# An attention and MLP kernel: the first batch opens with two query tiles of 128, its later queries load behind the values, and ties in the instruction order are broken by a hash

## The chip, the cores and the metric

The kernel runs on one core of one Trainium2 chip. The metric is device time in microseconds of one execution, 278.24 us before the change (median of 3 runs, 277.3 to 278.42). The core has TensorE (matrix products, PE in the profile), VectorE (DVE), ScalarE (ACT), GpSimd (POOL) and the queue engine SyncE (SP); loads can be issued from SP, ACT and POOL.

## The reference, cut to what matters

Four batches of eight heads, 768 tokens, head size 64. Attention under a block mask, then an MLP with a squared relu over all 3072 tokens.

```python
scores = scale * np.matmul(q, k.transpose(0, 1, 3, 2))          # q, k, v: (4, 8, 768, 64) f32
mask = np.abs(blk_i - blk_j) <= window                          # blocks of 32, window 1
mask = mask | (blk_i == 0) | (blk_j == 0) | (blk_i == n_blocks - 1) | (blk_j == n_blocks - 1)
... # and 3 sampled key blocks for each query block
scores = np.where(mask, scores, -1000000000.0)
attn = softmax(scores)                                          # written out in the reference
x = (attn @ v).transpose(0, 2, 1, 3).reshape(3072, 512)
h = x @ w_in                                                    # (512, 2048)
r = np.maximum(h, 0.0)
g = r * r
return (g @ w_out).astype(np.float32)                           # (2048, 512)
```

## The kernel before

Heads are taken in pairs; a pair of a batch is a unit `u` (16 units, 4 of each batch). A unit's keys lie on the partitions, 128 at a time, so scores come out as keys x queries, go through the exponential on ScalarE and are the stationary operand of the product with the values; a column of ones in the values gives the row sums. Queries are taken 256 at a time:

```python
QW = 256
def scores(slots, add, e):                    # one slot: unit u, query tile qi, key chunks 2*cp and 2*cp+1
    for a in slots:
        u, qi, cp = a
        ps = ps_s.tile([P, 2, 2, QW], F32, name="ps", tag="ps")          # two of these in all
        for c in range(2):
            for h in range(2):
                nc.tensor.matmul(ps[:, h, c, :], QK[i][hs, 1, ksl], QK[i][hs, 0, qsl], ...)   # L359
            for h in range(2) if add else ():
                nc.tensor.matmul(ps[:, h, c, :], oh[hs, ksl], R2[hs, qsl], ...)   # L363: adds the mask
def exps(a, e):
    A.activation(out=pT, in_=stile.pop(a), func=AF.Exp, scale=scale)     # L369
def masks(a, e):
    V.tensor_tensor(out=pT, in0=pT, in1=m[...], op=AOP.mult)             # L376: where no mask was added
def values(a, e):
    nc.tensor.matmul(po[:, qc, h, :], pT[:, h, c, ...], VT[i][:, h, n, 0:VW], ...)   # L392
def normalize(u, qi, e): ...                  # L399 and L401, VectorE
```

In batch 0 the first query tile has its mask added in the scores by TensorE; for the others a mask of zeros and ones is multiplied in by VectorE. The attention result is transposed (by TensorE in batch 0, by DMA later) into `xT`, and the MLP takes it tile by tile: 256 tokens in batch 0, 384 later.

```python
TILES = [(0, qi * QW, QW) for qi in range(NQ)]
TILES += [(b, c0, S // 2) for b in range(1, B) for c0 in (0, S // 2)]
def hidden(T, f, half, e):                    # ph, L437: 4 matmuls for one f of 16
    nc.tensor.matmul(ph, w_in_sb[:, kc, f * P:(f + 1) * P], xT[b][:, kc, c0:c0 + w], ...)
def relu(T, f, e): ...                        # r, VectorE (L446) or ScalarE (L444)
def square(T, f, e): ...                      # g, GpSimd (L455) or ScalarE (L453)
def output(T, i, ts, cs, part, e):            # py, L477: 2 of 16 f in each part
    nc.tensor.matmul(ytile[T, i], gtile[T, f][:, ts * P:(ts + 1) * P], w_out_sb[:, f, cs[0]:cs[1]], ...)
```

Loads of batch 0 are issued at the start from SP and ACT, whole tensors of 384 KB. The weights come in 8 chunks, 4 of w_in and 4 of w_out, issued by GpSimd; a copy on GpSimd in front of them holds them back until the keys of unit 2 have landed. Three tiny stores on SP ("gates") wait each for a weight chunk and so hold back the loads of the next batch that stand behind them.

```python
load(0, (sy, sc_, sy))                        # queries, keys, values: from SP, ACT, SP
load(1, (sc_, sy, sc_))
load(2, (sy, sc_, sy))
load(3, (sc_, sy, sy))
def w_load(i, e):
    if i == 0:
        G.tensor_copy(out=held, in_=raw[2][1][0:1, 0, 0, 0:2])           # keys of unit 2
    G.dma_start(out=w_in_sb[:, :, fs], in_=wiv[:, :, fs])                # or a chunk of w_out
def loads_gate(i, e):                         # i = 2 (w_in), 5 and 7 (w_out)
    sy.dma_start(out=scratch[0:1, i % 4:i % 4 + 1], in_=src)             # src lies in weight chunk i
```

The order of the instructions on each engine is made ahead, when the kernel is built: every piece of work is a task with durations, dependencies, buffers and a key; of those that could start earliest the one with the smallest key is taken. Twelve matmuls on a constant (`junk`, L223) run at the start. Identity, one-hot rows `oh` and the mask rows `bm` are made on GpSimd and VectorE.

Of the kernel before, what the change touches and what calls it, by code (L numbers as in the profile page):

```python
# [19 lines left out]
P = 128  # L20
# [5 lines left out]
def kernel(  # L26
# [31 lines left out]
    N_WARM = 12  # L58
# [16 lines left out]

    tasks = []
# [3 lines left out]
    AHEAD = {"PE": 0, "DVE": 0, "ACT": 0.2, "POOL": 0.0, "SP": 0.0}  # L80
    LEAD = 14
    PACE0, PACE, SINGLE, MASK_AT = 44, 1.313, 1, 12.0

    class Buf:
        def __init__(self, pool):
            self.pool, self.holds, self.free = pool, 0, 0.0

    class Task:
        def __init__(self, engs, key, fn, deps=(), get=(), put=(), after=0.0, mode=None, dma=0.0, late=None, bias={}, port=False):
            self.engs = engs if isinstance(engs, dict) else dict([engs])  # L90
            self.key, self.fn = key, fn
            self.deps, self.get, self.put = list(deps), list(get), list(put)
            self.after, self.mode, self.dma, self.late, self.bias = after, mode, dma, late, bias
            self.port = port
            self.end = self.eng = None
            self.order = len(tasks)
            for b in self.put:
                b.holds += 1
            tasks.append(self)
# [99 lines left out]

    sy, sc_ = nc.sync, nc.scalar  # L200
    sb_i = consts.tile([nb, n_rand * 2], I32, name="sb_i")
    sy.dma_start(out=sb_i, in_=sampled_blocks.bitcast(I32))
    load(0, (sy, sc_, sy))
    load(1, (sc_, sy, sc_))
    load(2, (sy, sc_, sy))
    load(3, (sc_, sy, sy))
# [7 lines left out]
    warm = consts.tile([P, 512], BF, name="warm")  # L214
# [7 lines left out]
    for _ in range(N_WARM):  # L222
        nc.tensor.matmul(junk, warm[:, 0:P], warm, start=True, stop=True)  # L223
# [7 lines left out]
    G.iota(row, pattern=[[0, 1]], base=0, channel_multiplier=1, **small)  # L231
    o3 = oh.rearrange("a (n p) -> a n p", p=P)
# [4 lines left out]
    identb = consts.tile([P, P], BF, name="identb")  # L237
    make_identity(nc, identb)
# [19 lines left out]
    A.copy(out=oh[D:P, :], in_=oh[0:D, :])  # L258
# [13 lines left out]
    def mask_rows(e):  # L272
        mtile["R"] = ps_s.tile([P, 1024], F32, name="pb", tag="ps")
        for c0 in (0, 512):
            w = min(512, S - c0)
            nc.tensor.matmul(mtile["R"][:, c0:c0 + w], bm, oh[0:nb, c0:c0 + w], start=True, stop=True)

    def mask_rows_evac(c0, c1, e):
        copy(e, R2[:, c0:c1], mtile["R"][:, c0:c1])
# [15 lines left out]
    mtile, cast, ttile = {}, {}, {}  # L295

# [31 lines left out]
    def w_load(i, e):  # L328
        if i == 0:
            G.tensor_copy(out=held, in_=raw[2][1][0:1, 0, 0, 0:2])  # L330
# [18 lines left out]
    def scores(slots, add, e):  # L349
        for a in slots:  # L350
            u, qi, cp = a
            i = u % NPB
            ps = ps_s.tile([P, 2, 2, QW], F32, name="ps", tag="ps")
            qsl = slice(qi * QW, (qi + 1) * QW)
            for c in range(2):
                ksl = slice((cp * 2 + c) * P, (cp * 2 + c + 1) * P)
                for h in range(2):
                    hs = slice(h * D, (h + 1) * D)
                    nc.tensor.matmul(ps[:, h, c, :], QK[i][hs, 1, ksl], QK[i][hs, 0, qsl],  # L359
                                     start=c == 0, stop=not add, skip_group_check=True)  # L360
                for h in range(2) if add else ():
                    hs = slice(h * D, (h + 1) * D)
                    nc.tensor.matmul(ps[:, h, c, :], oh[hs, ksl], R2[hs, qsl],  # L363
# [3 lines left out]
    def exps(a, e):  # L367
        pT = work.tile([P, 2, 2, QW], BF, name="pT", tag="pT", bufs=PT_BUFS)
        A.activation(out=pT, in_=stile.pop(a), func=AF.Exp, scale=scale)  # L369
        ptile[a] = pT  # L370

    def masks(a, e):
        u, qi, cp = a
        pT = ptile[a]
        m = MK[:, cp * 2:cp * 2 + 2, qi * QW:(qi + 1) * QW]
        V.tensor_tensor(out=pT, in0=pT, in1=m[:, None].broadcast_to([P, 2, 2, QW]), op=AOP.mult)  # L376

    def outs_of(t):
        return t[:, 0:4 * VW].rearrange("p (c h d) -> p c h d", h=2, d=VW)

    def values(a, e):
        u, qi, cp = a
        i = u % NPB
        pT = ptile.pop(a)
        if cp == 0:
            otile[u, qi] = ps_o.tile([P, 512], F32, name="po", tag="po")
        po = outs_of(otile[u, qi])
        for c in range(2):
            n = cp * 2 + c
            for qc in range(2):  # L390
                for h in range(2):
                    nc.tensor.matmul(po[:, qc, h, :], pT[:, h, c, qc * P:(qc + 1) * P], VT[i][:, h, n, 0:VW],  # L392
# [3 lines left out]
    def normalize(u, qi, e):  # L396
        po = outs_of(otile[u, qi])
        rs = work.tile([P, 2, 2, 1], F32, name="rs", tag="rs")
        V.reciprocal(out=rs, in_=po[:, :, :, D:VW])  # L399
        xq = work.tile([P, 2, 2, D], BF, name="xq", tag="xq", bufs=XQ_BUFS)  # L400
        V.tensor_tensor(out=xq, in0=po[:, :, :, 0:D], in1=rs.broadcast_to([P, 2, 2, D]), op=AOP.mult)  # L401
        xtile[u, qi] = xq

    def x_transp(u, qi, e):
        xq = xtile.pop((u, qi))
        pt = otile[u, qi][:, 384:512].bitcast(BF)
        for qc in range(2):
            nc.tensor.transpose(pt[:, qc * P:(qc + 1) * P], xq[:, qc].rearrange("p h d -> p (h d)"), identb)  # L408

    def x_evac(u, qi, e):  # L410
# [3 lines left out]
        copy(e, xT[b][:, a, qi * QW:(qi + 1) * QW], otile.pop((u, qi))[:, 384:512].bitcast(BF))  # L414

    def x_transp_dma(u, qi, e):
        b, a = divmod(u, HP)
        if b not in xT:
            xT[b] = work.tile([P, HP, S], BF, name="xT", tag="xT", bufs=XT_BUFS)
        sy.dma_start(out=xT[b][:, a, qi * QW:(qi + 1) * QW].rearrange("r (c p) -> r c p", p=P),  # L420
                     in_=xtile.pop((u, qi)).rearrange("p c h d -> p (c h d)"), transpose=True)
        otile.pop((u, qi))
# [4 lines left out]
    TILES = [(0, qi * QW, QW) for qi in range(NQ)]  # L427
    TILES += [(b, c0, S // 2) for b in range(1, B) for c0 in (0, S // 2)]
    NY = 8

    def hidden(T, f, half, e):
        b, c0, w = T
        if half == 0:
            htile[T, f] = ps_h.tile([P, TWM], F32, name="ph", tag="h")[:, 0:w]
        ph = htile[T, f]
        for kc in range(half * KM // 2, (half + 1) * KM // 2):
            nc.tensor.matmul(ph, w_in_sb[:, kc, f * P:(f + 1) * P], xT[b][:, kc, c0:c0 + w],  # L437
                             start=(kc == 0), stop=(kc == KM - 1))

    def relu(T, f, e):  # L440
        r = work.tile([P, TWM], F32, name="r", tag="r", bufs=R_BUFS)[:, 0:T[2]]
# [7 lines left out]
    def square(T, f, e):  # L449
        g = work.tile([P, TWM], BF, name="g", tag="g", bufs=G_BUFS)[:, 0:T[2]]  # L450
# [5 lines left out]
        gtile[T, f] = g  # L456
# [33 lines left out]
    def T_(engs, key, f, *args, **kw):  # L490
        return Task(engs, key, (lambda e: f(*args, e)), **kw)

    arrive = [(6.2, 6.2, 8.4), (8.4, 10.5, 10.5), (12.5, 12.5, 13.6), (13.6, 15.2, 16.3)]

    order = [(a, qi, cp) for qi in range(NQ) for a in range(HP) for cp in range(CP)]
    order += [(b * HP + a, qi, cp) for b in range(1, B) for qs in ((0, 1), (2,)) for a in range(HP) for qi in qs
              for cp in range(CP)]
    first = {}
    for s, (u, qi, cp) in enumerate(order):
        first.setdefault(u, s)  # L500
    ev, cv, tr, sc_of, va_of, mu, mk, wl, gate, xb = {}, {}, {}, {}, {}, {}, {}, {}, {}, {}

    def prepare(u):
# [5 lines left out]
        if u >= HP:  # L509
# [4 lines left out]
            for w in (1, 0):  # L514
                qc = Buf("qc")
                c = T_({"DVE": 0.55, "POOL": 1.2}, 101, cast_qk, u, w, slice(0, NCH), bias={"POOL": 0.5}, get=[qc], port=True,
                       after=PACE0 + PACE * (s0 - HP * NQ * CP) - LEAD, **at)
                tr[u].append(c)
                ev[u][w, 0] = ev[u][w, 2] = T_(("SP", 1.0), s0 - 10, transp_dma, u, w, deps=[c] + old_s, put=[qc], dma=1.2)
        else:  # L520
            at = dict(after=arrive[u][2])
            for ns in (slice(0, 2), slice(2, NCH)) if u == 0 else (slice(0, NCH),):
                n = ns.stop - ns.start
                for w in (0, 1):
                    qc, hb = Buf("qc"), Buf("h")
                    opts = {"ACT": 0.23 + 0.1 * n} if u == 0 and w else {"DVE": 0.07 + 0.08 * n}
                    if u:
                        opts["POOL"] = 1.2
                    c = T_(opts, s0 - 6 + ns.start, cast_qk, u, w, ns, after=arrive[u][w], get=[qc], port=True)
                    tr[u].append(c)  # L530
                    t = T_(("PE", 0.06 * n), s0 - 5 + ns.start, transp, u, w, ns, deps=[c], get=[hb], put=[qc], mode=128)
                    opts = {"DVE": 0.14 + 0.07 * n}
                    if u == 0:
                        opts["ACT"] = 0.23 + 0.1 * n
                    x = T_(opts, s0 - 4 + ns.start, evac, u, w, ns, deps=[t], put=[hb])
                    for j in range(ns.start, ns.stop, 2):
                        ev[u][w, j] = x
            for w in (0, 1):
                ev[u].setdefault((w, 2), ev[u][w, 0])
        cv[u] = [T_({"POOL": 0.83, "DVE": 0.55}, s0 - 2 if u < HP else 101, cast_v, u, bias={"DVE": 0.6},  # L540
                    deps=at.get("deps", []) + old_v, after=at.get("after", 0.0), port=True)]
        if u == HP - 1:
            for i in range(2 * NWP):
                wl[i] = T_(("POOL", 0.85), -50 + i, w_load, i, after=12.6, late=2.2, dma=2.65)
# [3 lines left out]
    def attend(group, add):  # L548
        s = min(order.index(a) for a in group)
        bufs = {a: Buf("ps") for a in group}  # L550
        sc = T_(("PE", (0.44 if add else 0.22) * len(group)), s, scores, group, add,
                deps=[ev[u][w, 2 if n else 0] for u, qi, cp in group for w, n in ((0, qi), (1, cp))]
                + (mr[:1 + (group[0][1] > 0)] if add else []) + sc_all[-1:], get=[bufs[a] for a in group], mode=64,
                after=PACE0 + PACE * (s - HP * NQ * CP) if s >= HP * NQ * CP else 0.0)
        sc_all.append(sc)
        for a in group:
            u, qi, cp = a
            sc_of[u].append(sc)
            s = order.index(a)
            pt = Buf("pT")  # L560
# [132 lines left out]
```

The softmax here doesn't subtract the row's maximum and nothing guards it: scores larger than these inputs give would overflow.

## Time and profile before

| | |
|---|---|
| time, median of 3 runs | 278.24 us |
| span of the profiled execution | 275.2 us |
| TensorE busy | 263.5 us, 96% |
| ScalarE busy | 212.0 us, 77% |
| VectorE busy | 198.0 us, 72% |
| GpSimd busy | 77.3 us, 28% |
| HBM read, written | 27.26 MB, 6.29 MB |

How to read it: the row of busy shares is over the whole span, and the stages differ. The view of busy time by stretches has one line for each stretch, with the busy time of PE, PEld (weight loads), DVE, ACT and POOL in this order, the number of instructions in brackets, then the granted clock of TensorE, the mean share of the 16 DMA engines and GB/s. A line of the timeline of an engine has start, length, engine, line of the kernel, operation, output and input, shapes, and the number of instructions merged; in brackets what the engine was idle for before it and what ended that. SPq and POOL lines with DMA_DIRECT2D are issues of a transfer, not the transfer.

### The profile page before, as it was taken

How to read it: one execution, taken by the hardware profiler on the slowest of the kernel's cores; microseconds unless marked ns; L12 is line 12 of the kernel's file. 1: busy time of each engine (PE TensorE's matmuls, PEld its weight loads, DVE VectorE, ACT ScalarE, POOL GpSimd, SP SyncE). 2: the span in 40 equal slices, each digit the busy share in tenths (PEclk: the TensorE clock that was granted, in tenths of full speed). 3: DMA queues.
4: the chain of work that ended last, by engine and by line, in shares of the span. 5: the costliest groups of instructions: out<-in, count | busy, mean ns of one | idle time of the engine just before them, and what ended most of it. 6: DMA issues, size and time to landing. Idle time of an engine off the chain costs nothing.

```text
span 275.2 us, 7001 instructions
## 1 busy us (share of the span) xinstructions
PE 263.5 (96%) x2812; PEld 156.7 (57%) x2850; DVE 198.0 (72%) x392; ACT 212.0 (77%) x315; POOL 77.3 (28%) x105
## 2 busy tenths in 40 slices
PE   7897999899999999999999999999999999999994
PEld 2565756567666655655555555555555655555543
DVE  6794799989989778898987768876876745444400
ACT  4688999899899799997898988889989743444311
POOL 4660655625441224453232420111110100010010
PEclk9999999999999999999999999999999999999999
DMA  7999997999979969413512611111022011111122
GB/s 251 376 233 206 267 278 252 262 280 285 318 104 255 206 174 247 154 57 69 117 48 48 137 21 50 57 21 49 12 60 58 12 48 39 40 38 38 40 76 76
DMA packets 50522, 36.89 MB, mean 134 GB/s; under 512 B 30906, under 2 KB 47546, under 8 KB 50490
## 3 DMA queue, kind: packets, MB, share of 16 engines
q1 hardware_dynamic: 44906, 30.29, 41.3%
q0 software_dynamic: 4224, 4.19, 9.2%
q10 hardware_dynamic: 1360, 1.97, 2.1%
q8 instruction: 22, 0.36, 0.5%
q14 instruction: 10, 0.08, 0.1%
HBM read 27.26 MB, written 6.29 MB: 122 GB/s over the span
## 4 chain that ended last, share of the span: by engine, by line
PE 87%; DVE 4%; ACT 3%; DMA 2%; issue 2%; POOL 1%; POOLq 0%; ACTq 0%
PE ph L437 28%; PE py L477 28%; PE po L392 14%; PE ps L359 12%; DMA vs<-in_v_dram 2%; ACT pT L369 2%; PE junk L223 2%; DVE pT L376 1%; PE pt L311 1%; DVE r L446 1%; POOL g L455 1%; DVE QK L182 1%; PE po L408 1%; PE ps L363 0%; ACT MK L291 0%
## 5 line engine op out<-in xcount | busy, mean ns | idle before, releaser
L369 ACT ACTIVATE pT<-ps 128x1024 bf16<-128x1024 f32 x144 | 139.2, 1022 | 9.0 <-PE ps L359 5.6
L437 PE MATMUL ph<-xT,w_in_sb 128*128 128x384 bf16 (+1 forms) x576 | 107.0, 308 | 0.2
L376 DVE TENSOR_TENSOR pT<-pT,MK 128x1024 bf16<-128x1024 bf16 x132 | 98.8, 769 | 10.5 <-ACT pT L369 10.3
L477 PE MATMUL py<-w_out_sb,g 128*128 128x512 bf16 (+1 forms) x362 | 96.2, 369 | 2.5 <-POOL g L455 0.9
L455 POOL TENSOR_TENSOR g<-r 128x256 bf16<-128x256 f32 (+1 forms) x59 | 50.0, 853 | 164.5 <-DVE r L446 134.6
L437 PEld LDWEIGHTS <-w_in_sb 128*128 128x128 bf16 x576 | 51.9, 97 | 33.0 <-issue 1.3
L446 DVE TENSOR_SCALAR r<-ph 128x384 f32<-128x384 f32 (+1 forms) x96 | 49.6, 519 | 28.5 <-PE ph L437 27.2
L453 ACT ACTIVATE g<-r 128x384 bf16<-128x384 f32 (+1 forms) x85 | 42.3, 501 | 29.2 <-DVE r L446 28.5
L392 PEld LDWEIGHTS <-pT 128*128 128x128 bf16 x1152 | 44.4, 98 | 22.4 <-issue 7.7
L392 PE MATMUL po<-VT,pT 128*128 128x65 bf16 x1152 | 53.9, 194 | 1.5 <-DVE xT L182 0.7
L477 PEld LDWEIGHTS <-g 128*128 128x128 bf16 x400 | 36.3, 97 | 24.7 <-POOL g L455 1.2
L359 PE MATMUL ps<-QK 64*128 64x256 bf16 x576 | 46.6, 272 | 0.1
L359 PEld LDWEIGHTS <-QK 64*128 64x128 bf16 x576 | 22.8, 94 | 24.1 <-issue 20.7
L444 ACT ACTIVATE r<-ph 128x384 f32<-128x384 f32 (+1 forms) x48 | 21.0, 445 | 5.3 <-PE ph L437 4.7
L401 DVE TENSOR_TENSOR xq<-po,rs 128x256 bf16<-128x256 f32 x48 | 20.4, 424 | 1.7
L399 DVE RECIPROCAL rs<-po 128x4 f32<-128x4 f32 x48 | 8.6, 180 | 17.9 <-PE po L392 17.6
L180 ACT COPY ys<-py 128x512 f32<-128x512 f32 (+1 forms) x21 | 11.9, 565 | 11.7 <-PE py L477 11.7
L182 POOL CAST VT<-vs 128x768 bf16<-128x768 f32 x15 | 13.5, 902 | 17.9 <-PE po L392 12.1
L182 DVE CAST qc<-ks 128x768 bf16<-128x768 f32 x14 | 9.5, 682 | 0.0
L182 DVE CAST qc<-qs 128x768 bf16<-128x768 f32 (+2 forms) x13 | 8.6, 666 | 0.8 <-DMA qs<-in_q_dram 0.8
L363 PE MATMUL ps<-R,oh 64*128 64x256 bf16 x48 | 5.9, 269 | 0.0
L223 PE MATMUL junk<-warm 128*128 128x512 bf16 x12 | 4.2, 528 | 1.5 <-DVE warm L215 1.5
(52 smaller groups left out, 61.3 us busy)
## 6 DMA issues: line engine op xcount, KB each, us to landing
out_dram<-ys SPq DMA_DIRECT2D x23, 256.0 KB, 2.2
vs<-in_v_dram SPq DMA_DIRECT2D x15, 384.0 KB, 6.4
qs<-in_q_dram SPq DMA_DIRECT2D x14, 384.0 KB, 4.5
ks<-in_k_dram SPq DMA_DIRECT2D x14, 384.0 KB, 6.4
w_in_sb<-in_moe_w_in_dram POOLq DMA_DIRECT2D x4, 512.0 KB, 10.1
w_out_sb<-in_moe_w_out_dram POOLq DMA_DIRECT2D x4, 512.0 KB, 20.7
ks<-in_k_dram ACTq DMA_DIRECT2D x2, 384.0 KB, 6.0
qs<-in_q_dram ACTq DMA_DIRECT2D x2, 384.0 KB, 5.0
```

The costliest lines, as they stand in the source:

```text
L182: (V if e == "DVE" else G).tensor_copy(out=out, in_=in_)
L359: nc.tensor.matmul(ps[:, h, c, :], QK[i][hs, 1, ksl], QK[i][hs, 0, qsl], start=c == 0, stop=not add, skip_group_check=True)
L369: A.activation(out=pT, in_=stile.pop(a), func=AF.Exp, scale=scale)
L376: V.tensor_tensor(out=pT, in0=pT, in1=m[:, None].broadcast_to([P, 2, 2, QW]), op=AOP.mult)
L392: nc.tensor.matmul(po[:, qc, h, :], pT[:, h, c, qc * P:(qc + 1) * P], VT[i][:, h, n, 0:VW], start=(n == 0 and qc == 0 and h == 0), stop=n ...
L401: V.tensor_tensor(out=xq, in0=po[:, :, :, 0:D], in1=rs.broadcast_to([P, 2, 2, D]), op=AOP.mult)
L437: nc.tensor.matmul(ph, w_in_sb[:, kc, f * P:(f + 1) * P], xT[b][:, kc, c0:c0 + w], start=(kc == 0), stop=(kc == KM - 1))
L444: A.activation(out=r, in_=src, func=AF.Relu)
L446: V.tensor_scalar(out=r, in0=src, scalar1=0.0, scalar2=None, op0=AOP.max)
L453: A.activation(out=g, in_=r, func=AF.Square)
L455: (G if e == "POOL" else V).tensor_mul(out=g, in0=r, in1=r)
L477: nc.tensor.matmul(ytile[T, i], gtile[T, f][:, ts * P:(ts + 1) * P], w_out_sb[:, f, cs[0]:cs[1]], start=(f == 0), stop=(f == NF - 1))
```

## The change

In batch 0 the first 256 queries become two tiles of 128, each slot with three key chunks instead of two (128 x 768 exponentials instead of 128 x 1024), so that the first MLP tile has its input after half as many queries. Both tiles have the mask added by TensorE, as the 256-query tile had before. For a 128-query tile the hidden layer takes two f at once, so that relu and square keep their 256 columns. Loads of batch 0 are cut: of the queries only the first 256 come early, the rest stands behind the last values, and the weights are held back by the values of unit 2 instead of its keys. Keys of unit 0 come in two parts. Identity is made before the one-hot rows; 24 more matmuls on the constant are put where TensorE is expected to wait; constants of the task order change, and every key gets an offset from a hash of the task's number.

```diff
-    N_WARM = 12
+    N_WARM, N_IDLE = 15, 24
+    QT0, ADDED, ALONE = [(0, 128), (128, 128), (256, 256), (512, 256)], (0, 128), (0, 128)
-    PACE0, PACE, SINGLE, MASK_AT = 44, 1.313, 1, 12.0
+    PACE0, PACE, SINGLE, MASK_AT = 35.961, 1.493, 1, 17.0
+    TIES = 515867, 2.374, 2.488
+            self.key += TIES[1 if key < 300 else 2] * tie(self.order)
...
-    load(0, (sy, sc_, sy))
-    load(1, (sc_, sy, sc_))
-    load(2, (sy, sc_, sy))
-    load(3, (sc_, sy, sy))
+    for eng, u, w, ns in ((sc_, 0, 1, KEYS[0]), (sy, 0, 0, QRS[0]), (sc_, 1, 1, ALL), (sy, 0, 1, KEYS[1]),
+                          (sc_, 1, 0, QRS[0]), (sy, 0, 2, ALL), (sc_, 1, 2, ALL), (sy, 2, 1, ALL),
+                          (sy, 2, 0, QRS[0]), (sy, 3, 1, ALL), (sy, 3, 0, QRS[0]), (sy, 2, 2, ALL), (sy, 3, 2, ALL),
+                          (sy, 0, 0, QRS[1]), (sy, 1, 0, QRS[1]), (sy, 2, 0, QRS[1]), (sy, 3, 0, QRS[1])):
+        load_part(eng, u, w, ns)          # w: 0 queries, 1 keys, 2 values
...
-    warm = consts.tile([P, 512], BF, name="warm")
+    warm = consts.tile([P, 256], BF, name="warm")
...                                       # identity moved ahead of the two selects on oh
-    A.copy(out=oh[D:P, :], in_=oh[0:D, :])
+    V.tensor_copy(out=oh[D:P, :], in_=oh[0:D, :])
...
+    idle = ps_y.tile([P, 512], F32, name="idle", tag="y")
+    def keep_warm(e):
+        nc.tensor.matmul(idle[:, 0:256], warm[:, 0:P], warm, start=True, stop=True)
...
-            G.tensor_copy(out=held, in_=raw[2][1][0:1, 0, 0, 0:2])
+            G.tensor_copy(out=held, in_=raw[2][2][0:1, 0, 0, 0:2])
...                                       # scores, exps, masks, values, normalize: by start and width
-    TILES = [(0, qi * QW, QW) for qi in range(NQ)]
+    TILES = [(0, c0, w) for c0, w in QT[0]]
+    def per_unit(T):
+        return 2 if T[2] == P else 1
...                                       # hidden, relu, square take per_unit(T) values of f at once
+    KEYS_OF = {P: [tuple(range(CP)), tuple(range(CP, NCH))], QW: [(2 * c, 2 * c + 1) for c in range(CP)]}
```

## The prediction

> **What bounds the kernel now.** I read the busy shares first, then the busy time by stretches, then the chain that ended last, and last the order of work on each engine in the first 60 us, where the change lies.
>
> ```profile
> PE 263.5 (96%) x2812; PEld 156.7 (57%) x2850; DVE 198.0 (72%) x392; ACT 212.0 (77%) x315; POOL 77.3 (28%) x105
> ```
> ```profile
> 20.00:25.00 5.00, 4.44 (x83) 3.00 (x80) 1.62 (x5) 4.48 (x6) 0.00 (x0) 1.00 1.24 207
> ...
> 50.00:60.00 10.00, 9.09 (x121) 6.17 (x122) 8.56 (x19) 9.18 (x15) 5.86 (x7) 1.00 1.21 238
> ...
> 100.00:150.00 50.00, 49.52 (x570) 28.48 (x577) 43.31 (x79) 45.00 (x65) 19.13 (x21) 1.00 0.45 109
> 150.00:200.00 50.00, 49.58 (x558) 28.17 (x564) 37.59 (x73) 44.41 (x62) 7.98 (x10) 1.00 0.22 53
> ```
>
> From 60 us on TensorE is busy over 98% of every stretch: only less TensorE work can shorten that part. To see what is lost earlier I priced all TensorE work at its steady pace, from the chain: hidden matmuls 8 in 0.87 us (256 wide) and 4 in 0.65 (384), output 8 in 1.73 (512), values 16 in 0.59, scores 8 in 0.54; transposes 0.06 each. With the counts of the program: hidden 83.3, output 82.9, values 42.6, scores with added masks 42.1, transposes and mask tiles 6.4, together 257.4 us. I then laid that running sum beside the start times of the weight loads (2850 of 2851 are recorded). Time minus work done, "lost" below, is 5.7 us at the first useful matmul, 7.1 at 7.8 us, 8.9 at 20, 11.1 at 28, 11.4 at 37, 12.6 at 43, 14.0 at 52, and still 14.0 at 271.3 us, the last matmul. So **after 52 us nothing is lost**; span = 257.4 + 14.0 + 3.9 for the last store. All the change can win is part of the 14.0.
>
> The loss has three parts. Until 8 us the data and the masks aren't there. From 8 to 28 us scores wait for ScalarE's exponentials and there is no hidden work to fill in:
>
> ```profile
> 8.77 2.88 ACT L369 ACTIVATE pT<-ps 128x1024 bf16<-128x1024 f32 x3 [1.65 <-PE ps L363]
> ...
> 18.41 5.61 ACT L369 ACTIVATE pT<-ps 128x1024 bf16<-128x1024 f32 x6 [1.30 <-PE ps L363]
> ```
> ```profile
> 27.64 1.71 PE L437 MATMUL ph<-xT,w_in_sb 128*128 128x256 bf16 x12
> ```
>
> The hidden layer starts at 27.64 us, when four head pairs times three exponentials are through. From 35 to 50 us VectorE and ScalarE are both over 90% busy in every 5 us, and from 37 to 52 us 2.6 us more go. Beside all this runs the DMA, saturated to 41 us:
>
> ```profile
> 11.07 0.17 POOL L330 COPY held<-ks 1x2 f32<-1x2 f32 x1 [0.92 <-DMA ks<-in_k_dram]
> 11.20 3.36 POOL L333 DMA_DIRECT2D w_in_sb<-in_moe_w_in_dram  x4
> 14.54 2.98 POOL L336 DMA_DIRECT2D w_out_sb<-in_moe_w_out_dram  x4
> ```
> ```profile
> 23.88 0.25 SPq L343 DMA_DIRECT2D scratch<-w_in_sb  x1
> ...
> 34.69 0.24 SPq L343 DMA_DIRECT2D scratch<-w_out_sb  x1
> ...
> 41.39 0.24 SPq L343 DMA_DIRECT2D scratch<-w_out_sb  x1
> ```
>
> These small stores are gates: each goes out the moment a weight chunk has landed. So w_in chunk 2 is there at 23.9 us, w_out chunk 1 at 34.7, w_out chunk 3 at 41.4. The packet records give all eight: 18.5, 21.0, 23.6, 26.3 (w_in), 29.6, 34.4, 37.6, 41.1 (w_out). Chunks alone take 2.55 us; w_out 1 took 4.7 because batch 1's first loads, let go by the gate at 23.9, ran beside it.
>
> [...] Here chunk w_in 2's last packet ended at 22.6 and its semaphore came at 23.6, so 1.0. [...] The trace has 216 at 512 (8 in 1.73 us). [...]
>
> **The change part by part.**
> (1) *TensorE work.* Hidden for the two 128-query tiles: 128 matmuls at 0.06 [...] = 7.7 for 64 x 0.109 = 7.0: +0.7. Scores and added masks: 192 of 128 columns, two side by side, at 0.03 (half of 0.055, the pace of a 256-wide one with masks) = 5.8 for 96 x 0.0675 = 6.5: -0.7. Sum 0. The 24 idle matmuls (0.108 each, 2.6 us) stand where the order expects TensorE to wait.
> (2) *Opening.* First keys 196 KB and queries 131 KB instead of 393 KB each; identity built before the selects; no table load behind a fifth load on ScalarE's queue. First scores near 6.2 us instead of 8.12, loss there 5.8 instead of 7.3: -1.5.
> (3) *Exponentials.* 128x512 took 0.60 us and 128x1024 took 1.02, so 128x768 takes 0.81, in a row 0.73 against 0.935. The first hidden matmul stands behind about 14 of them: 14 x 0.73 = 10.2, copies and masks on ScalarE 1.2, waits for keys of pairs 1 to 3 about 2, from 6.9 us: 20.3, plus 0.7 to the matmul: 21.0 us. Work ahead of it is 13.0 us, so the loss is 8.0 there, against 11.1 before. Up to here **3.1 us are won**.
> (4) *Weights.* Here I expect most of it to be given back. The weights are now held by the values of pair 2. Bytes ahead of those and with them: 4.72 MB of loads less 0.39 and 1.05 = 3.28 MB, at the 0.35 MB/us of the loads before (4.72 MB from 1.9 to 15.4 us): 11.3, landed 11.7, then their cast on GpSimd 0.9: first weight issue about 12.7 instead of 11.2. Before, chunk 0 shared 0.8 us with the last value load; now it doesn't. Net **1.1 us later** for every chunk: 19.6, 22.1, 24.7, 27.3, 30.7, 35.5, 38.7, 42.2. The order of the changed program gives the work ahead of each first use, and landing minus work is the least loss: w_in 0 19.6 - 13.0 = 6.6; w_in 1 22.1 - 14.6 = 7.5; w_in 2 24.7 - 16.5 = 8.2; w_in 3 27.3 - 18.0 = 9.3; w_out 0 30.7 - 19.6 = 11.1; **w_out 1 35.5 - 22.9 = 12.6**; w_out 2 38.7 - 28.9 = 9.8; w_out 3 42.2 - 31.2 = 11.0. Before, w_out 1's first use had 24.75 us of work ahead and came at 36.3, after its landing. So the earlier start of the hidden layer runs into the weights, w_out 1 above all, and the loss there is 12.6.
> (5) *After that.* From 35.5 us to batch 1's first scores there are 24.3 us of TensorE work; ScalarE has 16 exponentials (15.0), 14 relu or squares (4.9) and 2.9 of masks and copies = 22.8; VectorE about as much (18 mask products 11.9, normalizing 3.4, the rest 7.5). Both fit, barely; before they didn't, and 2.6 us went. I put 0.5 on it. Loss at 60 us: 13.1, against 14.0.
> (6) *Later.* Between a score tile and the use of its buffer by the next but one lie 2.6 us of TensorE work in the median, before and after, so the rest should stay without loss, though ties fall otherwise. The tail is the same, 3.9.
>
> Sum: 278.24 - (14.0 - 13.1) = **277.3 us**.
>
> **The rivals.**
> A: *the weights don't bind.* If batch 1's loads leave w_out 1 its bandwidth, it lands at 33 or before, and the loss grows only from 8.0 by what remains of the later waits, to 10.5 or 11: 275. For it: gaps in the DMA may hide the shift. Against: its mean share is over 1.0 in every 5 us from 5 to 40 us.
> B: *small pieces cost.* Four more exponentials, eight more normalizing pairs, split casts and idle matmuls in the wrong place, on engines that are full from 30 us: loss 15 to 16: 279.5. For it: VectorE was over 95% busy from 35 to 50 us. Against: it has only 1.62 us of work between 20 and 25 us, which the earlier hidden layer fills.
> C: *the shaken order stalls later*, after 60 us, where before nothing was lost: +1 to 2, so 279. No line speaks for it, and buffer distances speak against.
>
> **Range and chances.** I give my reading 0.55, A 0.25, B and C 0.2: 275.2 to 279.3. Over 2% faster needs 272.7, a loss of 8.4 in all, which is what I expect already at the first hidden matmul: 0.05. Over 2% slower needs 283.8, 5.6 lost anew: 0.03.
>
> **What would show it.** Right: first exponential near 7 us; first hidden matmul near 21; TensorE waiting at the first output matmuls for w_out chunks, with the gate stores near 25, 35.8 and 42.5 us; TensorE over 98% busy after 60. Wrong: gates at the old times or before; TensorE under 97% in a stretch after 70 us (C); ScalarE or VectorE without idle time at 35 to 60 us while TensorE waits for them (B). A loss at 60 us under 11 would refute step 4.

## The result and the profile after

The changed kernel takes 277.41 us (median of 4 runs, 277.26 to 277.54) against 278.31 for the kernel before measured beside it. The ratio is 0.9976, with a 95% interval from 0.9951 to 1.0: a gain between nothing and half a per cent. The kernel before, run again beside each group of experiments, had medians of 277.74, 278.06 and 277.89 us (29 to 57 runs), so part of the 0.9 us between the medians may belong to these few runs. The predicted 277.3 us is within 0.1 us of the result, but the way there was another one than predicted.

The busy shares of the kernel after, first, and then its busy time by stretches (PE, PEld, DVE, ACT, POOL, granted clock, DMA share, GB/s):

```profile
PE 268.5 (97%) x3037; PEld 164.2 (60%) x3037; DVE 197.5 (72%) x388; ACT 216.4 (79%) x330; POOL 92.0 (33%) x116
```
```profile
20.00:25.00 5.00, 5.00 (x104) 3.40 (x101) 3.70 (x11) 4.96 (x8) 0.90 (x2) 1.00 1.24 207
...
50.00:60.00 10.00, 9.59 (x125) 6.13 (x120) 9.39 (x18) 9.04 (x14) 6.30 (x7) 1.00 1.06 313
...
100.00:150.00 50.00, 50.00 (x565) 29.16 (x563) 40.12 (x71) 46.32 (x69) 22.63 (x23) 1.00 0.47 109
150.00:200.00 50.00, 50.00 (x564) 29.12 (x563) 37.79 (x71) 45.34 (x65) 11.86 (x12) 1.00 0.28 58
```

TensorE is busy for 5 us more than before and the time is hardly shorter: busy time contains the idle matmuls, and the narrow ones count for more than they cost (a pair of score matmuls 128 wide is shown as 0.22 us below, though the pairs start 0.055 us apart). From 20 to 25 us the row says 5.00 of 5.00, and yet 0.7 us were lost there by the prediction's measure, time minus priced work. That measure, taken in the same way at the same moments:

| lost, us, at | 8 | 16 | 24 | 28 | 36 | 40 | 44 | 52 | 60 | 100 | 270 |
|---|---|---|---|---|---|---|---|---|---|---|---|
| before | 7.2 | 8.2 | 9.9 | 11.0 | 11.4 | 11.9 | 12.6 | 13.9 | 13.7 | 13.8 | 14.0 |
| before, a second execution | 7.6 | 8.9 | 10.3 | 11.9 | 12.3 | 12.3 | 13.5 | 14.1 | 14.9 | 14.9 | 15.0 |
| after | 7.2 | 10.5 | 12.0 | 12.2 | 12.9 | 13.0 | 13.3 | 13.9 | 14.4 | 14.7 | 14.6 |

Two kernels of the experiments (late gates, and late gates with keys first) differ from the changed one only from 25 us on, so their openings are two more executions of its opening: losses of about 9.4 and 10.3 us at 16 us, 10.9 and 11.7 at 28. One program's opening can thus differ by 1.3 us between executions. With that spread nothing is won in the opening: at 16 us the changed kernel is behind in all three, at 28 us it has 10.9 to 12.2 against 11.0 and 11.9 before, and it ends between the two executions of the kernel before. Its tail after the last matmul is about 3.5 us, 3.9 before. Now the engines in the opening of the kernel after, ScalarE first; in brackets what it was idle for, and what ended that:

```profile
8.02 0.81 ACT L398 ACTIVATE pT<-ps 128x768 bf16<-128x768 f32 x1 [1.12 <-PE ps L391]
10.42 0.81 ACT L398 ACTIVATE pT<-ps 128x768 bf16<-128x768 f32 x1 [1.59 <-PE ps L391]
11.52 1.54 ACT L398 ACTIVATE pT<-ps 128x768 bf16<-128x768 f32 x2 [0.28 <-PE ps L391]
...
14.10 0.81 ACT L398 ACTIVATE pT<-ps 128x768 bf16<-128x768 f32 x1 [0.36 <-PE ps L391]
15.55 4.79 ACT L398 ACTIVATE pT<-ps 128x768 bf16<-128x768 f32 x6 [0.64 <-PE ps L391]
```

Before, three exponentials stood in a row from 8.77 us. Here most of the first ones wait for their scores. On TensorE of the kernel after:

```profile
5.18 1.06 PE L323 MATMUL idle<-warm 128*128 128x256 bf16 x4
6.03 0.42 PE L339 MATMUL pt<-identb,qc 128*128 128x128 bf16 x2
...
7.47 0.23 PE L387 MATMUL ps<-QK 64*128 64x128 bf16 x2
...
25.15 0.38 PE L474 MATMUL ph<-xT,w_in_sb 128*128 128x128 bf16 x4
...
34.78 0.39 PE L474 MATMUL ph<-xT,w_in_sb 128*128 128x128 bf16 x4
...
36.14 0.59 PE L515 MATMUL py<-w_out_sb,g 128*128 128x512 bf16 x2 [0.97 <-DMA w_out_sb<-in_moe_w_out_dram]
```

The first hidden matmul starts at 25.15 us, 2.5 us sooner than before. But only 13.0 us of work lie ahead of it, where before some 16.6 did: nothing gained. At 36.14 us the output layer waits for weights, as predicted. The gates and the hold in front of the weights of the kernel after, on SyncE and on GpSimd:

```profile
25.67 0.25 SPq L371 DMA_DIRECT2D scratch<-w_in_sb  x1
...
36.11 0.24 SPq L371 DMA_DIRECT2D scratch<-w_out_sb  x1
...
44.82 0.24 SPq L371 DMA_DIRECT2D scratch<-w_out_sb  x1
```
```profile
13.54 0.50 POOL L358 COPY held<-vs 1x2 f32<-1x2 f32 x1
13.99 2.66 POOL L361 DMA_DIRECT2D w_in_sb<-in_moe_w_in_dram  x3
```

By the packet records the eight chunks are there at 19.8, 22.7, 25.3, 27.8, 30.9, 35.7, 39.9 and 44.4 us. The first six are within 0.6 us of the forecast, and the last two 1.2 and 2.2 us later.

### The profile page after: what moved, and what is told of

Same layout as the page of the kernel before. It is cut to its first block, busy times and chain, and to the rows that moved or that the text cites. A ratio compares the mean times of both kernels' runs of the same rounds, so it can differ in the third digit from the quotient of the medians.

```text
span 275.5 us, 7465 instructions
## 1 busy us (share of the span) xinstructions
PE 268.5 (97%) x3037; PEld 164.2 (60%) x3037; DVE 197.5 (72%) x388; ACT 216.4 (79%) x330; POOL 92.0 (33%) x116
## 4 chain that ended last, share of the span: by engine, by line
PE 86%; DMA 6%; DVE 6%; POOL 1%; ACT 0%; issue 0%; DVEq 0%; ACTq 0%
PE py L515 29%; PE ph L474 28%; PE po L420 13%; PE ps L387 12%; DMA w_out_sb<-in_moe_w_out_dram 6%; DVE pT L405 3%; PE junk L248 1%; DVE qc L195 1%; PE idle L323 1%; PE pt L339 1%; DVE r L483 0%; DVE xq L430 0%; PE ps L391 0%; DVE R L195 0%; ACT pT L398 0%
## 5 line engine op out<-in xcount | busy, mean ns | idle before, releaser
L398 ACT ACTIVATE pT<-ps 128x1024 bf16<-128x1024 f32 (+1 forms) x148 | 140.5, 1001 | 11.9 <-PE ps L387 7.3
L405 DVE TENSOR_TENSOR pT<-pT,MK 128x1024 bf16<-128x1024 bf16 x132 | 105.8, 825 | 13.3 <-ACT pT L398 13.2
L474 PE MATMUL ph<-xT,w_in_sb 128*128 128x384 bf16 (+2 forms) x640 | 107.7, 294 | 0.0
L492 POOL TENSOR_TENSOR g<-r 128x256 bf16<-128x256 f32 (+1 forms) x68 | 61.4, 908 | 129.6 <-DVE r L483 83.0
L483 DVE TENSOR_SCALAR r<-ph 128x384 f32<-128x384 f32 (+1 forms) x73 | 38.1, 523 | 29.4 <-PE ph L474 28.8
L387 PE MATMUL ps<-QK 64*128 64x256 bf16 (+1 forms) x624 | 47.5, 264 | 0.2 <-ACT pT L398 0.2
L481 ACT ACTIVATE r<-ph 128x384 f32<-128x384 f32 (+1 forms) x71 | 31.0, 453 | 4.9 <-PE ph L474 4.6
L430 DVE TENSOR_TENSOR xq<-po,rs 128x256 bf16<-128x256 f32 (+1 forms) x52 | 21.0, 404 | 1.8
L193 ACT COPY ys<-py 128x512 f32<-128x512 f32 (+1 forms) x21 | 11.9, 565 | 13.0 <-PE py L515 12.8
L428 DVE RECIPROCAL rs<-po 128x4 f32<-128x4 f32 (+1 forms) x52 | 9.1, 176 | 15.7 <-PE po L420 15.5
L391 PE MATMUL ps<-R,oh 64*128 64x128 bf16 x96 | 7.1, 216 | 0.0
## 6 DMA issues: line engine op xcount, KB each, us to landing
w_out_sb<-in_moe_w_out_dram POOLq DMA_DIRECT2D x4, 512.0 KB, 12.8
```

The costliest lines, as they stand in the source:

```text
L387: nc.tensor.matmul(ps[:, h, j * w:(j + 1) * w], QK[i][hs, 1, ksl], QK[i][hs, 0, qsl], start=j == 0, stop=not add, skip_group_check=True)
L398: A.activation(out=pT[:, :, 0:n], in_=stile.pop(a)[:, :, 0:n], func=AF.Exp, scale=scale)
L474: nc.tensor.matmul(htile[T, f][:, i * w:(i + 1) * w], w_in_sb[:, kc, f_ * P:(f_ + 1) * P], xT[b][:, kc, c0:c0 + w], start=(kc == 0), stop= ...
L481: A.activation(out=r, in_=src, func=AF.Relu)
L483: V.tensor_scalar(out=r, in0=src, scalar1=0.0, scalar2=None, op0=AOP.max)
L492: (G if e == "POOL" else V).tensor_mul(out=g, in0=r, in1=r)
```

## The experiments

Each is an edit of the changed kernel, if nothing else is said; ratios are to the kernel before, run beside it. "Loss" is the measure of the table. Two explanations stand against each other. **Weights**: what the opening wins is taken back at w_out chunk 1. **Chain**: the opening wins nothing to begin with, because casts, transposes and copies, in the order set for each engine, stand between the loads and the scores, whatever the tile. Beside them stand the hash, the idle matmuls and the hold of the weights, each of which may have its own part.

### The kernel before, once more

No edit: it tells how far one profile of it can be trusted.

> The kernel before once more, for a second profile. In the two profiles at hand the changed kernel has a span 0.3 us longer than the one before, while the medians say 0.9 us shorter. Reading 1: the profiled execution of before was a lucky one (276.95 us beside a median of 278.31); a second profile then shows about 1.0 us more lost before 60 us (15.0 instead of 14.0) and a span near 276.5. Reading 2: the loss of before is 14.0 in all its executions, and the gain lies outside of the span; then the second profile shows 14.0 again. Time 278.3 in both.

277.53 us, ratio 0.9994 [0.9974, 1.0014]. The second execution profiled took 277.93 us with a span of 276.2, the first 276.95 with 275.2. ScalarE of the second one:

```profile
9.45 2.86 ACT L369 ACTIVATE pT<-ps 128x1024 bf16<-128x1024 f32 x3 [1.65 <-PE ps L363]
```

Its first exponential starts 0.7 us later than in the first execution (8.77), and its loss ends at 15.0, not 14.0. The loss of 14.0 that the prediction counted from was that of an execution 1.3 us under the median to which the result was then added.

### Without the idle matmuls

```diff
     def keep_warm(e):
-        nc.tensor.matmul(idle[:, 0:256], warm[:, 0:P], warm, start=True, stop=True)
+        pass
```

> The changed kernel with its 24 idle matmuls left out, everything else in the same order. Theory of the feed (the opening is set by keys landing and their way through VectorE, later by the landing of w_out chunk 1): the first scores come up to 0.8 us earlier, the loss at the first hidden matmul falls from 12.1 by at most 1, w_out chunk 1 still lands at 35.7 us and the time stays at 277.0 to 277.6. Rival (the idle matmuls cost time on the path): 276.3 to 276.7, with the gain still there at 60 us. Second rival [...]: slower by 0.5 to 1.

277.43 us, 0.9997 [0.9982, 1.0012]. On TensorE:

```profile
6.25 0.29 PE L387 MATMUL ps<-QK 64*128 64x128 bf16 x2
...
34.44 0.39 PE L474 MATMUL ph<-xT,w_in_sb 128*128 128x128 bf16 x4
...
36.23 0.38 PE L515 MATMUL py<-w_out_sb,g 128*128 128x512 bf16 x1 [1.41 <-DMA w_out_sb<-in_moe_w_out_dram]
```

The first scores come 1.2 us sooner than in the profile of the changed kernel, at the predicted 6.2: there four idle matmuls at 5.18 us had stood among the first transposes. In two other executions of that opening, idle matmuls included, the first scores came at 6.64 us (late gates) and 7.18 us (keys first), so the idle ones cost them 0.4 to 1.2 us. But the loss at 16 us is 10.3 (after: 10.5), and at 36 us 12.9, the same. What was still ahead at 34 us is paid as a longer wait for w_out chunk 1, 1.41 us for 0.97. Between 34.8 us and the end of that wait TensorE starts no matmul; the four hidden matmuls that stand behind it in the order start at 36.66 us, after it.

### Batch 1's loads let go later

The gates wait for w_out chunks 1 and 3 instead of w_in chunk 2 and w_out chunk 1; the order on every engine stays.

```diff
     def loads_gate(i, e):
+        at, i = i % 4, {2: 5, 5: 7}.get(i, i)
...
-        sy.dma_start(out=scratch[0:1, i % 4:i % 4 + 1], in_=src)
+        sy.dma_start(out=scratch[0:1, at:at + 1], in_=src)
```

> The changed kernel with the loads of batch 1's first unit let go by w_out chunk 1 instead of w_in chunk 2, and those of the second by w_out chunk 3; all orders the same. Theory of the weights (w_out chunk 1 lands late because the first unit's loads share its bandwidth): it lands at 33.0 to 33.5 us instead of 35.7, the wait for it in front of the output matmuls is gone, the loss at 37 us falls from 13.3 to 12.3 to 12.6, and the time by 0.4 to 1.0, to 276.4 to 277.0. Rival (VectorE and ScalarE bind from 30 to 60 us): the wait is gone but the loss at 60 us is 14.9 as before, time 277.2 to 277.6. If the first unit's keys now come too late for VectorE's order, slower: 278 and more.

276.81 us, 0.9966 [0.9952, 0.9981]. W_out lands at 30.0, 32.5, 35.5 and 38.7 us, chunk 1 3.2 us sooner than after. TensorE and VectorE of this kernel:

```profile
33.66 0.38 PE L516 MATMUL py<-w_out_sb,g 128*128 128x512 bf16 x1
...
41.77 0.29 PE L438 MATMUL po<-identb,xq 128*128 128x128 bf16 x2 [1.35 <-DVE xq L431]
```
```profile
40.60 0.56 DVE L195 CAST qc<-ks 128x768 bf16<-128x768 f32 x1 [2.15 <-DMA ks<-in_k_dram]
```

The wait for weights is gone, and the loss at 36 us is 10.6 instead of 12.9. Not all of that is the edit's: this execution stood at 10.9 us of loss already at 28 us, 1.3 less than the profile of the changed kernel, though the gates act only from 25.7 us on. Its six exponentials in a row started 1.5 us sooner, in the same program:

```profile
14.04 4.95 ACT L399 ACTIVATE pT<-ps 128x768 bf16<-128x768 f32 x6 [0.59 <-PE ps L392]
```

From 28 to 36 us the loss fell by 0.3 here and grew by 0.7 there: about 1 us is what the late gates won. VectorE stands 2.15 us, until 40.6 us, at the cast of batch 1's first keys, which now come late. An attention normalization is held behind it: its reciprocal starts at 41.08 us, after the cast, though the products with the values ahead of it on TensorE ended at 39.56 us. TensorE stands 1.35 us behind that. Loss 12.4 at 44 us, 13.5 at the end: the wait was moved from the weights to the keys. By the time alone this kernel isn't told from the changed one (0.9966 and 0.9976, with intervals that overlap).

### The first tile as before, 256 wide

```diff
-    QT0, ADDED, ALONE = [(0, 128), (128, 128), (256, 256), (512, 256)], (0, 128), (0, 128)
+    QT0, ADDED, ALONE = [(0, 256), (256, 256), (512, 256)], (0,), (0,)
```

> The changed kernel with one opening tile of 256 queries in place of the two of 128 (loads, hash and constants as changed; the order is made anew). Theory of the feed: small tiles use up a pair's keys before the next pair's are ready, so with 256 the loss at 16 us falls from 10.6 to 8.0 to 9.0, the first hidden matmul stays at 25 to 27 us, and the time is 276.9 to 278.0. Rival (the small tiles bring the gain of 0.9): 278.2 to 278.8.

277.18 us, 0.9991 [0.997, 1.0013]. The first hidden matmul is at 27.16 us with 16.2 us of work ahead. The loss is 9.1 at 16 us and 10.8 at 28, less than in the profile of the small tiles (10.5 and 12.2) but as in the execution of their opening with late gates (9.4 and 10.9), and 14.7 at the end. The tiles of 128, the first thing that the change names, make no difference to the time that these runs can tell.

### Late gates, with the order made anew for them

```diff
-            g = gate[2] if u == HP else gate[5] if u == HP + 1 else gate[7]
+            g = gate[5] if u == HP else gate[7]
...
-            for i in (2, 5, 7):
+            for i in (5, 7):
```

> The changed kernel with the same late gates as in the run before (first unit of batch 1 let go by w_out chunk 1, the rest by w_out chunk 3), but with the order made anew, so that VectorE's and GpSimd's casts of these loads stand where the data is there. Theory of the weights: no wait for w_out chunk 1, and not the wait of 2.15 us for the late keys either that the same order had; loss 12 to 12.6 at 40 us and 13 at 60; time 276.0 to 276.6, below the 276.8 of the late gates alone. Rival (VectorE and ScalarE give the loss at 60 us): 14 or more at 60 us, 277 and over.

276.93 us, 0.9982 [0.9964, 1.0]: less than expected. GpSimd and TensorE of this kernel:

```profile
48.62 0.85 POOL L195 CAST VT<-vs 128x768 bf16<-128x768 f32 x1 [4.71 <-DMA vs<-in_v_dram]
```
```profile
50.40 0.61 PE L515 MATMUL py<-w_out_sb,g 128*128 128x512 bf16 x2 [0.23 <-POOL g L492]
```

The loss stays at 12.1 to 12.8 from 48 to 56 us and is then 14.1 at 60. In the new order it is GpSimd that waits for late loads: 9.7 us in four waits for values, the longest shown above, and its squares stand behind the casts. TensorE in turn waits for a square at 50.40 us.

### Without the hash

```diff
-    TIES = 515867, 2.374, 2.488
+    TIES = 515867, 0.0, 0.0
```

> The changed kernel with the hash's weight set to 0 in both places, the order made anew. The first use of w_out chunk 1 then has 24.3 us of work ahead instead of 22.9, so the wait for it should be gone, but w_out chunk 3 at 42.5 has 29.1 ahead, a least loss of 13.4. Theory of the weights: loss at 60 us 14.0 to 15.0, time 277.0 to 278.0, the same as with the hash. Rival (the hash holds the gain): 278.3 to 279.

279.48 us, 1.0053 [1.0034, 1.0072]. I had taken the hash for noise. Without it the same kernel is some 2 us slower. Its loss at 28 us is 11.7, near that of the kernel after (12.2); then it grows to 15.0 at 48 us and 16.7 at the end. One of its waits on TensorE, late in the program:

```profile
154.24 1.02 PE L515 MATMUL py<-w_out_sb,g 128*128 128x512 bf16 x4 [0.90 <-DVE ys L195]
```

Here an output copy on VectorE stood too far back in the order. The other constants (pace, lead, readiness) had come with the hash in one change, and it isn't known what they would be without it.

### Another seed for the hash

```diff
-    TIES = 515867, 2.374, 2.488
+    TIES = 1, 2.374, 2.488
```

> The changed kernel with another seed of the hash (1 in place of 515867). Without a hash it took 279.5 us. If breaking ties by any hash helps, 277.0 to 278.0. If the seed was picked together with the other constants and another one is as good as none, 278.5 to 280.

277.49 us, 1.0001 [0.9982, 1.002]. TensorE of this kernel:

```profile
31.68 0.59 PE L515 MATMUL py<-w_out_sb,g 128*128 128x512 bf16 x2 [0.86 <-DMA w_out_sb<-in_moe_w_out_dram]
...
36.52 0.59 PE L515 MATMUL py<-w_out_sb,g 128*128 128x512 bf16 x2 [1.33 <-DMA w_out_sb<-in_moe_w_out_dram]
```

Another order, and in this execution a better opening: first hidden matmul at 23.6 us, loss 10.6 at 24 us against 12.0 (and 10.9 in the execution with late gates, so it need not be the order's doing). It then waits 2.2 us for two w_out chunks and stands at 12.9 at 36 us, as the kernel after does. This is the clearest case of the weights taking back what an opening had won. By the time, a seed taken without any search isn't told from the other one: 1.0001 and 0.9976, with intervals that just overlap.

### The weights held by keys again

```diff
-            G.tensor_copy(out=held, in_=raw[2][2][0:1, 0, 0, 0:2])
+            G.tensor_copy(out=held, in_=raw[2][1][0:1, 0, 0, 0:2])
...
-                wl[i] = T_(..., after=12.9 + 2.6 * i - (1.7 if i else 0), late=1.3, dma=2.6)
+                wl[i] = T_(..., after=9.5 + 2.6 * i - (1.7 if i else 0), late=1.3, dma=2.6)
```

> The changed kernel with the weights held by the keys of unit 2 as before the change, the order made anew with the weight issues ahead of the third value cast. They should be issued near 10 us instead of 14.0, run beside the last values and queries, and land at 18.5 to 19 (w_in 0) and 34.0 to 34.8 (w_out 1) instead of 19.8 and 35.7; the last values and queries land 1 us later. Theory of the weights: the loss at 37 us falls by 0.5 to 1.0; time 276.6 to 277.2. Theory of the feed: the opening loses what the weights win; 277.2 to 277.8.

279.13 us, 1.0061 [1.0038, 1.0084]. The profiled execution took 282.7, so only its order of events is used. GpSimd and VectorE of it:

```profile
10.02 1.68 POOL L361 DMA_DIRECT2D w_in_sb<-in_moe_w_in_dram  x2
```
```profile
15.72 0.43 DVE L195 CAST qc<-qs 128x512 bf16<-128x512 f32 x1 [1.13 <-DMA qs<-in_q_dram]
...
19.32 0.43 DVE L195 CAST qc<-qs 128x512 bf16<-128x512 f32 x1 [1.33 <-DMA qs<-in_q_dram]
```

My expectation was wrong. Weights issued 4 us sooner land no sooner: the first chunk at 19.55 us (after: 19.8) and the sixth at 35.73 (35.7). They are under way beside the rest of the queries, for which VectorE then waits four times, 0.86 to 1.33 us. Holding the weights behind the values is the right part of the change; in this remade order it is worth 1.7 us by the medians (279.13 and 277.41), and the ratios' intervals are apart.

### Late gates in the kernel before

The edit of "Late gates, with the order made anew", on the kernel before.

> The kernel before with the late gates alone (first unit of batch 1 by w_out chunk 1, the rest by w_out chunk 3). There the first use of w_out chunk 1 comes at 36.3 us, after its landing at 34.4. Theory of the weights: nothing waits for it, so nothing is won; ratio to before 0.999 to 1.003. Rival (late gates help any order, by leaving the DMA to the weights): 0.996 to 0.998 as in the changed kernel.

278.84 us, 1.0025 [1.0013, 1.0037]. SyncE and TensorE:

```profile
32.38 0.25 SPq L343 DMA_DIRECT2D scratch<-w_out_sb  x1
```
```profile
37.97 0.59 PE L477 MATMUL py<-w_out_sb,g 128*128 128x512 bf16 x2
```

Chunk w_out 1 lands at 31.95 us and TensorE asks for it 6 us later. Where the hidden layer starts late, sooner weights bring nothing. What the 0.25% went into isn't shown: the order was made anew, and from 30 to 62 us no engine waits over 0.5 us for a late load.

### Late gates, and keys ahead of queries

The queries of a later batch stood ahead of its keys and values in the queue; the keys are needed first, and now come first, then the values. Beside the edit of "Batch 1's loads let go later":

```diff
     def load(u, engs):
...
-        for name, view, eng in zip(("qs", "ks", "vs"), (qv, kv, vv), engs):
-            t = ld.tile([P, 2, NCH, D], F32, name=name, tag=name)
-            eng.dma_start(out=t.rearrange("p t n d -> p t (n d)"), in_=view[b, a])
-            raw[u].append(t)
+        for name in ("qs", "ks", "vs"):
+            raw[u].append(ld.tile([P, 2, NCH, D], F32, name=name, tag=name))
+        for w in (1, 2, 0):
+            engs[w].dma_start(out=raw[u][w].rearrange("p t n d -> p t (n d)"), in_=(qv, kv, vv)[w][b, a])
```

> The changed kernel with the late gates, all orders the same, and in the loads of batches 1 to 3 the keys first, the values next and the queries last (before: queries, keys, values). With late gates alone VectorE stood 2.15 us at the cast of the first unit's keys, and TensorE 1.35 us behind it. Theory of the weights: the keys land about 1 us earlier, the wait on VectorE falls under 1.2 us and TensorE's to under 0.5; loss at 44 us 0.5 to 1.5 lower than the 12.4 of the late gates; time 275.8 to 276.6. Rival: the wait moves to another engine and the time stays at 276.8.

276.01 us, 0.994 [0.9916, 0.9964]. VectorE and TensorE, the same two places as in the kernel with late gates alone:

```profile
39.59 0.56 DVE L195 CAST qc<-ks 128x768 bf16<-128x768 f32 x1
```
```profile
41.30 0.28 PE L438 MATMUL po<-identb,xq 128*128 128x128 bf16 x2
```

Both waits are gone. The loss is 11.6 at 36 us, 11.8 at 44 and 13.0 at the end, 1.6 less than after; at 28 us it was 11.7, so from there to 44 us nothing is lost, where the changed kernel lost 1.1. The time shows it without any profile: each of these 7 runs (275.23 to 276.59 us) is faster than all 28 runs of the two kernels with the early gates that ran in the same rounds (another seed, and unit 0's keys below: 276.68 to 278.82). Keys first with the early gates was not run, so the share of each of the two edits is not known.

### The same without idle matmuls

Both edits together: keys first with late gates, and no idle matmuls.

> The kernel of the run before (late gates, keys first) with the 24 idle matmuls left out as well. Leaving them out brought the first scores from 7.5 to 6.2 us in the changed kernel, and nothing of it was left at 36 us because of the wait for w_out chunk 1. Theory of the weights: with that wait gone some of it stays: 0.3 to 0.8 us under the run before. Rival (the opening is set by the later chain of casts and transposes, not by the first scores): the same within 0.2.

275.51 us, 0.9932 [0.9908, 0.9956]: the best of all, faster than the kernel before by 0.4 to 0.9%. Against the previous kernel the medians differ by 0.5 us, inside the intervals. The changed kernel wasn't run beside it; by the two ratios to the kernel before it is some 0.4% faster than that (0.9932 and 0.9976, whose intervals overlap by a hair).

### Unit 0's keys and queries for all of batch 0

```diff
-        copy(e, c, raw[u][w].rearrange("p t n d -> p n t d")[:, ns])
+        copy(e, c, raw[u if u >= HP else 0][w].rearrange("p t n d -> p n t d")[:, ns])
```

Units 1 to 3 compute with unit 0's keys and queries, so that none of them waits for its own; the loads stay. It leaves out the use of those units' own data.

> The changed kernel with the casts of units 1 to 3 in batch 0 reading unit 0's keys and queries, so that they wait for no later load; it leaves out the use of those units' own keys and queries (the loads still run, the order is the same, batch 0's output is another). It tells what makes the opening late. Arrival of keys: the loss at 16 us falls from 10.5 to under 9.5, and at 28 us from 12.2 to 11. Chain of casts, transposes and copies on engines that work in order: the loss at 16 us stays within 0.4 of 10.5. The time in both: 277.0 to 277.6, since w_out chunk 1 takes up what is won.

277.84 us, 1.0006 [0.9988, 1.0023]. ScalarE:

```profile
15.03 4.79 ACT L398 ACTIVATE pT<-ps 128x768 bf16<-128x768 f32 x6 [1.25 <-PE ps L391]
```

The six exponentials in a row start at 15.03 us instead of 15.55, and the loss at 16 us is 10.3 instead of 10.5. That is inside the spread of the opening (14.04 us and 9.4 with late gates, where every unit uses its own keys). And in the trace of the changed kernel no cast of the keys of units 1 to 3 on VectorE waits for a load. So it is not that these keys land late that makes the opening late, but what comes after the landing. Which link of it is not settled. The values were left as they were: GpSimd waits for them until 8.23 us and again until 12.77 us, so their landing isn't ruled out. Two more candidates were seen in the trace and not tested alone: casts of values on GpSimd beside casts on VectorE (last section), and a reciprocal on VectorE at 12.53 us that waits 1.58 us for the product with the values, with the copy of unit 2's keys behind it.

## Why the prediction was right or wrong

The time was right, 277.3 for 277.41, but by luck: the mechanism that was to win in the opening failed, so there was little for the weights to take back, and an error in the base made up for the rest.

1. *TensorE work, sum 0.* The pace held: score pairs of 128 columns start 0.055 us apart, as taken, and hidden matmuls of 128 columns 0.056 us apart, where 0.06 was my estimate. But the idle matmuls were not free where they stood: four from 5.18 us on were 0.21 us apart, among the transposes that the first scores need. As the run without them takes 277.43 us, this cost nothing in the end.
2. *Opening, -1.5.* Too early as built (first scores at 7.47, 6.64 and 7.18 us in three executions, not 6.2), right without idle matmuls (6.25). Even there it wasn't kept: the loss at 16 us was 10.3.
3. *Exponentials, first hidden matmul at 21.0 us, 3.1 us won.* **This step failed.** The time from 6.9 to 21.0 us was built of 10.2 + 1.2 + 2.0 + 0.7. Measured: sixteen score tiles stand ahead of the first hidden matmul on TensorE, and with two buffers for them the last one needs the fourteenth exponential to be done. The first exponential starts at 8.02 us, and the fourteenth ends at 23.27. That stretch holds 14 exponentials (11.2), copies and a mask tile on ScalarE (1.2) and waits for scores (2.9); then it is 1.9 us to the first hidden matmul at 25.15, for the order on TensorE has transposes, scores and values in between. So the start was 1.1 too early, the exponentials 1.0 too small (0.80 each in the row of six, not 0.73), the waits 0.9 and the last step 1.2; only the count of 14 and the 1.2 of copies held. The pace of ScalarE itself was right. The first of the six start at 15.55, 16.26 and 17.02 us, 0.71 and 0.76 apart; the one at 17.94 had to wait for scores that TensorE began at 17.33. With two score buffers and TensorE's other work between, the row is not ScalarE's alone. Loss 12.1 at that matmul, not 8.0; in the best execution of this opening (late gates) it was 10.9 at 28 us. "3.1 us are won" was refuted: nothing was that these profiles can tell from the 11.0 and 11.9 before.
4. *Weights, 1.1 us later.* Right in the first six landings (above), partly by luck: the first issue came at 13.99 us, not 12.7, and the first chunk shared the DMA with the late queries until 17.4 us, where the prediction had it share nothing. The run with the weights held by keys shows that the time of issue doesn't set the landing there (issued at 10.02, landed at 19.55). Right in the mechanism: w_out chunk 1 ends a wait of TensorE, and four kernels with a loss of 12.2, 11.5, 11.5 and 10.7 us at 28 us (after, no idle matmuls, unit 0's keys, seed 1) all stand at 12.8 or 12.9 at 36 us. As there was little to give back, it took only about 1 us here. The forecast loss of 12.6 at this point became 13.0 at 40 us, from a start that was wrong by 4.
5. *+0.5 until 60 us, loss 13.1.* It was 14.4 at 60 us, so 1.4 after 40 us. No single wait of TensorE there is over 0.33 us; what makes them up is not settled.
6. *No loss later, tail 3.9.* Right but for 0.2 us and some 0.4 us.

Rival A (275, weights don't bind) falls by the 0.97 us wait, and by the late gates with keys first, which remove it and gain. Rival B (small pieces on engines that are full from 30 us) falls too: the loss comes before 16 us, and the tile of 256 takes as long. Rival C (later stalls) shows in the order without the hash, in part: its loss grows by 1.1 us after 150 us.

The level came out right because of the base as well. The 14.0 us of loss belonged to an execution of 276.95 us and were used with a median of 278.24. The second profile of the kernel before, close to the median, has 15.0. With that base the forecast of 13.1 would have been a gain of 1.9 us and a time of 276.3. Between 14.0, 15.0 and 14.6, one execution each, the gain of 0.9 us in the medians can't be placed in any stage; it stays open which part of it is real.

## What to carry to other kernels

A gain in one stage counts only up to the next thing that comes at a fixed time: here eight weight chunks behind loads that fill the DMA (its share is 1.08 to 1.33 in every 5 us from 5 to 45 us of the kernel after). List the landing times, the work ahead of each first use, and look for the one that binds; then change the order of the transfers (later loads behind the weights, keys ahead of queries) before the start of the work. And before one profile is subtracted from, compare its time with the median: in this kernel two profiles of the same program differ by 1 us, and three of the same opening by 1.3 us, more than the change is worth.

## What the runs showed of the hardware

A cast of 128 x 256 on VectorE took 0.91 us while GpSimd cast values at 8.23 to 10.03 us, and 0.28 us just after. VectorE of the kernel after:

```profile
8.44 0.91 DVE L195 CAST qc<-qs 128x256 bf16<-128x256 f32 x1
...
10.67 0.28 DVE L195 CAST qc<-qs 128x256 bf16<-128x256 f32 x1
```

In the run with unit 0's keys the first of these casts ran at 7.94 us and took 0.29 us. No edit here separates the two engines, so what made it longer in the kernel after is not shown.

Part of the opening's matmuls ran at half pace, and when differed. In the kernel after, those of 256 columns were 0.21 us apart until about 6 us and about 0.11 us apart from 6.9 us on, and pairs of 128-column score matmuls 0.055 us apart from 7.5 us on; the granted clock is shown as 1.00 in all of this time. Without the idle matmuls such pairs were 0.10 to 0.11 us apart until about 10 us and 0.055 from 10.6 us on. With keys first and without idle matmuls they were 0.055 us apart from 6.5 to 9.0 us, 0.10 to 0.11 from 9.3 to 10.9 us, and 0.055 again from 13.0 us on. So it isn't shown that the idle matmuls bring the full pace forward, and the time of the kernel was the same (277.43 without and 277.41 with them): they were worth nothing here that these runs can tell.

Small packets of batch 0's loads cost somewhat more by the byte: in the median 512 B took 0.027 us, 768 B 0.036, 1024 B 0.048 and, in the kernel before, 1536 B 0.065. In the stores 2048 B took 0.086, and in the queue of the weights 1024 B took 0.098. The last packet of batch 0's loads ended at 17.4 us, against 15.4 before; but from 15.7 us on they shared the DMA with the first weights, so this isn't the price of the cut alone.
